# Unit 3 of a fused attention and feed-forward kernel takes the softmax-sum path of the units after it

## The chip, the cores and the metric

The kernel runs on one core of a Trainium2 chip. The metric is the device time of one execution in microseconds, given as the median of several runs. A profiled execution gives a span (first to last instruction) and a trace of every engine: TensorE (PE, with its weight loads shown as PEld), VectorE (DVE), ScalarE (ACT), GpSimd (POOL), and SyncE (SP), which only issues DMAs here.

## The reference

Attention with normalised queries and keys, for 8 batches of 12 heads, 448 tokens and 64 channels a head, and then two matrix products over the 3584 tokens:

```python
q_n, k_n = rmsnorm(q, g_q), rmsnorm(k, g_k)
scores = (1 / sqrt(64)) * q_n @ k_n.T
attn = exp(scores - max(scores))
attn = attn / (sum(attn) + 1e-9)
x = concat_heads(attn @ v)            # 3584 x 768
h = x @ w_in                          # 768 x 2048
out = maximum(0.01 * h, h) @ w_out    # 2048 x 768
```

## The kernel before

**Units and steps.** The work of attention is cut into 24 units (`NU`). A unit is four heads of one batch, so that three units make a batch; unit 3 is the first of batch 1. A unit's scores are computed transposed, as seven tiles of 128 keys by 2 x 448 (`et[:, t]`, t = 0 to 6). From unit 3 on, one loop (L963) runs over units `u` and four steps `d`: step 0 computes tile 0, steps 1 to 3 two tiles each (`STEPS`). Each tile is scored by PE into a *score slot* (`slot`, L194: two PSUM banks, two such slots in all), and ACT takes its exponential (`ex`, L218). The scores of step 0 also give the shift of the exponential: DVE takes a maximum over the tile (L236), spreads it on a diagonal `dg` (L238), a small PE matmul brings it to every partition (`shift_mm`), DVE takes the maximum of that (L249 or L255) and makes the bias `eb` (L257), for which the unit's first exponential waits.

**What closes a unit.** The closing of unit u-1 stands in step 0 of unit u. It has two forms, and `narrow(u-1)` chooses:

- The wide form (`zsum_slot`, `pv`, `zinv`, `xmul`), used before for units 0, 1, 3 and 23 (unit 2 has a variant of its own). The sums over the keys are computed by 64-row matmuls with a block of ones into a score slot, where each of 64 partitions gets the same sum (L280). PV goes to two of the four `aux` banks (L367). ACT makes the reciprocal of the sums with Ln and Exp over 128 x 896 (L353, L354), and DVE multiplies PV in PSUM by it, giving `xt`, the input of the first matrix product (L376).
- The narrow form (`pv_slot`, `zcol`, `pv_out`, `zcol_ln`, `zcol_inv`, `xmul_sb` or `xmul_pool`), used for units 4 to 22. PV goes to a score slot. The sums are computed by 32-column matmuls into one `aux` bank, as 128 x 224 (L307). The shift's matmul writes to the rest of PV's slot (L248). PV is copied to `x32` in SBUF, by DVE for units 4 to 6 and by ACT after that (L320, L322). ACT does Ln and Exp over 128 x 224 (L327, L332), and four DMAs on SyncE's queue spread the result to `rz`, 128 x 896 (L337). The product of `x32` and `rz` (L347) follows a unit or half a unit later, on DVE or on GpSimd.

**Added exponential tiles.** `add_e` (L292) lets DVE add up the first `ADDED[u]` exponential tiles of a unit in fp16. The sums then need `7 - ADDED[u] + 1` matmul groups instead of seven. `ADDED[3]` is 5: four additions, three groups.

**What sets the order.** Everything is issued in an order written by hand (`manual_schedule`); each engine takes its instructions in that order. The matrix products wait in `queue` as items of six to eight matmuls (`moe1`, L389, reading `xt`; `moe2` and `seven`, reading `gt`). `fill(u, d, jobs)` takes as many of them in each step as a digit of `PLAN` says ("1222" for unit 4) and places the step's `jobs` between them. In unit 4, step 0, `prep_tr` also transposes unit 5's normalised queries and keys on PE (L179); for units from 6 on that is a DMA transpose (`prep_trd`, L183), followed by a scaling on DVE (`prep_g`, L155).

**Preparing units ahead.** Unit u+4's rows are loaded by SyncE in step 0 (L125), their squares are made by GpSimd or ACT (L152, L148), reduced by DVE (L159), and normalised by DVE in step 2 (`prep_norm`, L171) two units ahead. SyncE's queue holds these loads, the `rz` DMAs, the DMA transposes and the stores, in program order. GpSimd's DMA queue holds the weights and the rows of v.

Of the kernel before, what the change touches and what calls it, by code (L numbers as in the profile page):

```python
# [18 lines left out]
def kernel(  # L19
# [18 lines left out]
    NU = B * NQ  # L38
# [163 lines left out]
    def qk(u, steps):  # L202
        st[u]["sT"] = []
        for t in steps:
            sT = slot()
            score(u, t, (sT[:, 0], sT[:, 1]))
            st[u]["sT"].append((t, sT))
# [17 lines left out]
    def shift_max(u):  # L225
        s = st[u]
        sT = s["sT"][0][1]
        if isinstance(sT, list):
            pm2 = small.tile([P, 2], FP32, tag="pm2", name="pm2")
            for a in range(2):  # L230
                nc.vector.tensor_reduce(pm2[:, a:a + 1], sT[a][:, 0:S], axis=AXL.X, op=ALU.max)
            s["spare"] = sT[0]
            nc.vector.tensor_reduce(s["spare"][:, 511:512], pm2, axis=AXL.X, op=ALU.max)
        else:
            s["spare"] = sT[:, 0]
            nc.vector.tensor_reduce(s["spare"][:, 511:512], sT[:, :, 0:S], axis=AXL.XY, op=ALU.max)  # L236
        s["dg"] = small.tile([P, P], FP16, tag="dg", name="dg")
        nc.vector.tensor_tensor(s["dg"], ident16, s["spare"][:, 511:512].broadcast_to([P, P]), op=ALU.mult)  # L238
# [4 lines left out]
    def shift_mm(u):  # L243
        s = st[u]
        if u > 0 and "pslot" in st[u - 1]:
            pb = st[u - 1]["pslot"][:, :, S:S + 64]
            for x in range(2):
                nc.tensor.matmul(pb[:, x], onesp, s["dg"][:, 64 * x:64 * x + 64], start=True, stop=True)  # L248
            nc.vector.tensor_reduce(s["spare"][:, 510:511], pb, axis=AXL.XY, op=ALU.max)  # L249
        else:  # L250
            if "pb" not in s:
                shift_bank(u)
            pb = s["pb"]
            nc.tensor.matmul(pb[:, 0:P], onesp, s["dg"], start=True, stop=True)
            nc.vector.tensor_reduce(s["spare"][:, 510:511], pb[:, 0:P], axis=AXL.X, op=ALU.max)  # L255
        s["eb"] = small.tile([P, 1], FP32, tag="eb", name="eb")
        nc.vector.tensor_scalar(s["eb"], s["spare"][:, 510:511], -1.0, DELTA, op0=ALU.mult, op1=ALU.add)  # L257
# [24 lines left out]

    HS = S // 2
    ADDED = {u: 4 for u in (7, 10, 11, 13, 16, 17, 19)}
    ADDED.update({3: 5, 4: 5, NU - 1: 5})
    ADDED.update({u: 3 for u in (8, 14, 20, 22)})

    def add_e(u):
        s = st[u]
# [9 lines left out]
    def zcol(u):  # L299
        s = st[u]  # L300
        s["zc"] = aux([P, 512], FP32, "zc")
        ets = z_tiles(u)
        for i, e in enumerate(ets):
            for y in range(2):
                for a in range(2):
                    c = 32 * (2 * y + a)
                    nc.tensor.matmul(s["zc"][c:c + 32, 0:HS], onesr, e[:, a, HS * y:HS * y + HS],  # L307
                                     start=(i == 0), stop=(i == len(ets) - 1))

    def pv_slot(u):  # L310
        s = st[u]
        s["pslot"] = slot()
        s["pv"] = [s["pslot"][:, r] for r in range(2)]
        pv(u)

    def pv_out(u):
        s = st[u]
        s["x32"] = zpool.tile([P, 2, S], FP32, tag="x32", name="x32")
        if u in (4, 5, 6):
            nc.vector.tensor_copy(s["x32"], s["pslot"][:, :, 0:S])  # L320
        else:
            nc.scalar.copy(s["x32"], s["pslot"][:, :, 0:S])  # L322

    def zcol_ln(u):
        s = st[u]
        s["zs"] = zpool.tile([P, HS], FP32, tag="zs", name="zs")
        nc.scalar.activation(s["zs"], s["zc"][:, 0:HS], AF.Ln)  # L327
        drop(s["zc"])
# [10 lines left out]
    def xmul_sb(u):  # L339
        xmul_pool(u, nc.vector)  # L340
# [74 lines left out]
    def flush(keep=False):  # L415
        kept = [p for p in pend if keep and p[0] in (s1, s2, s3, s4)]
        now = [p for p in pend if p not in kept]
        pend[:] = kept
        for fn, args in now:
            fn(*args)  # L420
# [312 lines left out]
    STEPS = ((0,), (1, 2), (3, 4), (5, 6))  # L733

    def narrow(u):
        return 4 <= u < NU - 1

    def fed(u, d):
        return u % NQ == 0 and d == 3
# [31 lines left out]
    with tc.manual_schedule():  # L771
# [191 lines left out]
        for u in range(3, NU):  # L963
            for d in range(4):
                if d > 0 or u > 3:
                    qk(u, STEPS[d])
                    if d == 0:
                        shift_max(u)
                        flush()
                        if u == 6:  # L970
                            xmul_sb(u - 2)
                        if narrow(u - 1):
                            pv_slot(u - 1)
                            zcol(u - 1)
                            shift_mm(u)
                            pv_out(u - 1)
                        else:
                            zsum_slot(u - 1)
                            pv(u - 1)
                            shift_mm(u)  # L980
                            zinv(u - 1)
                    ex(u)
                    if d == 0 and narrow(u - 1):
                        zcol_ln(u - 1)
                if d == 2 and ADDED.get(u, 0) > 3 and u < NU - 1:
                    add_e(u)
                    if u > 4:
                        xmul_sb(u - 1)
                jobs = []

                def job(fn, *args):
                    jobs.append(lambda: fn(*args))

                if d == 0:
                    if u == 3:
                        prep_norm(4)
                        gate(4)
                    elif narrow(u - 1):
                        if u < NU - 1:
                            job(zcol_inv, u - 1)  # L1000
                    else:
                        xmul(u - 1)
                    if u + 4 < NU:
                        job(load, u + 4)
                    if u + 3 < NU:
                        load_v(u + 3)
                    if u < 6:
                        prep_sqp(u + 3)
                if d == 1 and narrow(u - 1) and not 5 <= u < 8 and ADDED.get(u, 0) < 4:
                    xmul_pool(u - 1)  # L1010
                if u == NU - 1:
                    if d == 1:
                        job(zcol_inv, u - 1)
                if fed(u, d) and u > 3:
                    push(u // NQ - 1)
                if (u, d) in ((3, 1), (4, 0)):
                    for ti in range(2):
                        prep_tr(u + 1, ti, VV)
                if d == 1 and 5 <= u < NU - 1:
                    job(prep_g, u + 1)  # L1020
                if u + 2 < NU:
                    if d == 1:
                        if ADDED.get(u) == 3:
                            job(lambda u: (prep_ssq(u + 2), add_e(u)), u)
                        else:
                            for ti in range(2):
                                job(prep_ssq, u + 2, ALL, (ti,))
                    if d == 2:
                        job(prep_rinv, u + 2)
                        if u == 6:  # L1030
                            job(xmul_sb, u - 1)
                        for ti in range(2):
                            job(prep_norm, u + 2, ALL, (ti,))
                        if u > 3:
                            job(prep_trd, u + 2)
                if d == 1 and 4 <= u < 8:
                    job(weight_sum, u - 4, 0)
                if d == 0 and 5 <= u < 9:
                    job(weight_sum, u - 5, 1)
                if d == 1 and u == NU - 2:  # L1040
                    jobs.append(lambda: None)
                    job(add_e, u)
                if u == NU - 2 and d == 0:
                    for n, tile_ in ((1, (raws, "rq", 3)), (2, (raws, "rk", 3)), (3, None), (4, (prep_p, "sq", 3))):
                        job(win_sum, n, 1, tile_)
                    for n in (3, 1, 2, 4):
                        job(x_sum, LATE, n)
                if u == NU - 1 and d == 3:
                    job(add_e, u)
                    job(xmul_sb, u - 1)  # L1050
                if d == 3 and 6 <= u < NU - 3:
                    for ti in range(2):
                        job(prep_sq, u + 3, ALL, (ti,))
                fill(u, d, jobs)
# [39 lines left out]
```

## Time and profile before

| what | value |
|---|---|
| time, median of 3 runs | 415.95 us (415.69 to 416.95) |
| span of the profiled execution | 414.3 us |
| unit 4 begins (first score matmul) | 54.82 us |
| unit 5 begins | 68.90 us |
| unit 6 begins | 81.02 us |
| DVE busy 60.3 to 69.0 us | 8.30 of 8.70 us |
| ACT busy 60.3 to 69.0 us | 8.49 of 8.70 us |
| PE busy 60.3 to 69.0 us | 8.70 of 8.70 us |
| DMA for w_out, issue to landing | 23.5 and 33.0 us |

How to read it: the page gives each engine's share of the span, the chain of work that ended last, and groups of instructions by line. The timeline gives single instructions in order of time, with the idle time of the engine before each in brackets and what ended it. A busy engine is not always a bound: the stage around the change is what counts, and there the three compute engines are all nearly full.

### The profile page before, as it was taken

The page shows a single profiled execution, that of the slowest core. Times are in us where ns is not written, and L with a number is a line of the kernel's source. Part 1 is how long each engine was busy: PE and PEld are TensorE (multiplying, and loading weights), DVE is VectorE, ACT ScalarE, POOL GpSimd, SP SyncE. Part 2 cuts the span into 40 slices and gives each one's busy share as a digit, 9 for nine tenths or more (in the row PEclk, how much of TensorE's full clock was granted, in tenths as well). Part 3 has the DMA queues.
Part 4 walks back from the last instruction along what each step waited for, and adds up shares of the span by engine and source line. Part 5 has one row for each costly group of instructions (what it writes and reads, how often), then busy time and mean ns, then how long its engine had stood idle before and what let it go on. Part 6 is the DMA issues. An engine that isn't in the chain of part 4 may idle for free.

```text
span 414.3 us, 9374 instructions
## 1 busy us (share of the span) xinstructions
PE 399.1 (96%) x3831; PEld 219.6 (53%) x3831; DVE 308.7 (74%) x492; ACT 300.1 (72%) x470; POOL 68.4 (17%) x70
## 2 busy tenths in 40 slices
PE   8779999999999999999999999998999999999995
PEld 7445444454445544555445544454445557558863
DVE  5889798898788766767669757768568788658762
ACT  5989987667887699777987779866986657653600
POOL 1868422200020200020020200002002202000000
PEclk9999999999999999999999999999999999999998
DMA  5999999899765895677664796666562470032023
GB/s 178 290 239 251 241 250 177 207 170 214 140 156 89 221 239 92 159 194 157 163 151 77 211 212 133 171 157 128 194 112 47 120 149 18 9 77 76 2 56 97
DMA packets 71950, 62.41 MB, mean 151 GB/s; under 512 B 36324, under 2 KB 67044, under 8 KB 71908
## 3 DMA queue, kind: packets, MB, share of 16 engines
q1 hardware_dynamic: 61312, 49.62, 46.8%
q0 software_dynamic: 10272, 11.80, 18.2%
q8 instruction: 30, 0.49, 0.5%
q10 hardware_dynamic: 324, 0.39, 0.3%
q14 instruction: 12, 0.10, 0.1%
HBM read 45.61 MB, written 11.01 MB: 137 GB/s over the span
## 4 chain that ended last, share of the span: by engine, by line
PE 80%; DVE 10%; ACT 4%; DMA 2%; issue 2%; SPq 1%; DVEq 0%; ACTq 0%
PE hps L389 27%; PE sT L199 8%; PE op L435 5%; PE sT L367 5%; PE bank L602 5%; PE bank L476 5%; PE ma L476 5%; PE mc L476 4%; PE md L476 4%; DVE n L171 3%; ACT et L218 3%; PE mb L476 2%; PE zc L307 2%; PE sT L476 1%; DVE sT L236 1%
## 5 line engine op out<-in xcount | busy, mean ns | idle before, releaser
L218 ACT ACTIVATE et<-sT,eb 128x896 f16<-128x896 f32 x166 | 159.6, 1010 | 23.9 <-PE sT L199 13.9
L389 PE MATMUL hps<-xt,win 128*128 128x448 f16 x600 | 120.8, 353 | 0.2 <-DVE xt L376 0.2
L389 PEld LDWEIGHTS <-win 128*128 128x128 f16 x612 | 56.7, 98 | 58.3 <-issue 9.5
L383 ACT ACTIVATE gt<-hps 128x448 f16<-128x448 f32 x100 | 54.0, 557 | 4.7 <-PE hps L389 4.1
L199 PE MATMUL sT<-qkT 64*64 64x448 f16 x664 | 52.5, 363 | 3.0 <-ACT et L218 2.1
L159 DVE TENSOR_REDUCE ssq<-sq 128x14 f32<-128x896 f32 (+2 forms) x49 | 50.1, 1059 | 1.3 <-ACT sq L148 1.2
L476 PEld LDWEIGHTS <-sa 128*128 128x128 f16 x352 | 32.8, 98 | 26.4 <-issue 5.8
L128 POOL DMA_DIRECT2D vt<-in_v_dram x24 | 18.0, 748 | 169.3 <-PE sT L367 163.2
L322 ACT COPY x<-sT 128x896 f32<-128x896 f32 x16 | 14.5, 906 | 31.2 <-DVE sT L249 31.2
L476 PEld LDWEIGHTS <-gt 128*128 128x128 f16 x264 | 25.3, 98 | 18.4 <-issue 2.1
L199 PEld LDWEIGHTS <-qkT 64*64 64x64 f16 x672 | 15.3, 104 | 36.2 <-issue 32.0
L347 POOL TENSOR_TENSOR xt<-x,rz 128x896 f16<-128x896 f32 x9 | 18.7, 2082 | 81.7 <-DMA rz<-zs 73.5
L171 DVE TENSOR_TENSOR n<-rq,rinv 128x896 f16<-128x896 f32 (+2 forms) x25 | 28.7, 1149 | 3.4 <-ACT rinv L165 3.4
L236 DVE TENSOR_REDUCE sT<-sT 128x1 f32<-128x896 f32 x22 | 24.1, 1095 | 7.4 <-PE sT L199 7.3
L367 PE MATMUL sT<-et,vt 64*64 64x448 f16 x532 | 28.4, 349 | 0.0
L435 PE MATMUL op<-wout,gt 128*128 128x384 f16 x160 | 28.4, 327 | 0.0
L292 DVE TENSOR_TENSOR ea<-ea,et 128x896 f16<-128x896 f16 x27 | 16.9, 625 | 15.0 <-ACT et L218 13.7
L171 DVE TENSOR_TENSOR n<-rk,rinv 128x896 f16<-128x896 f32 (+2 forms) x26 | 26.2, 1012 | 0.0
L367 PEld LDWEIGHTS <-vt 64*64 64x64 f16 x672 | 20.1, 107 | 10.8 <-issue 0.4
L435 PEld LDWEIGHTS <-gt 128*128 128x128 f16 x192 | 17.7, 98 | 13.7 <-issue 3.1
L476 PE MATMUL ma<-wout,gt 128*128 128x384 f16 x128 | 23.5, 326 | 0.0
L292 DVE TENSOR_TENSOR ea<-et 128x896 f16<-128x896 f16 x14 | 9.4, 673 | 10.5 <-ACT et L218 10.5
(144 smaller groups left out, 550.5 us busy)
## 6 DMA issues: line engine op xcount, KB each, us to landing
rq<-in_q_dram SPq DMA_DIRECT2D x24, 448.0 KB, 3.9
rk<-in_k_dram SPq DMA_DIRECT2D x24, 448.0 KB, 5.0
out_dram<-ost SPq DMA_DIRECT2D x52, 192.0 KB, 3.2
rz<-zs SPq DMA_DIRECT2D x76, 112.0 KB, 2.3
vt<-in_v_dram POOLq DMA_DIRECT2D x24, 224.0 KB, 4.7
win<-in_moe_w_in_dram POOLq DMA_DIRECT2D x8, 384.0 KB, 13.8
wout<-in_moe_w_out_dram POOLq DMA_DIRECT2D x2, 1536.0 KB, 28.3
out_dram<-ost SPq DMA_DIRECT2D x4, 96.0 KB, 2.1
```

Of the source, the lines that this page charges most:

```text
L159: nc.vector.tensor_reduce(buf(u, "ssq")[:, ti, :, c[0]:c[1]], buf(u, f"sq{ti}")[:, :, c[0]:c[1]], axis=AXL.X, op=ALU.add)
L171: nc.vector.tensor_tensor(buf(u, "n16")[:, ti, c[0]:c[1]].rearrange("p s a d -> p a s d"), src[:, :, c[0]:c[1]], buf(u, "rinv")[:, ti, :, ...
L199: nc.tensor.matmul(banks[a][64 * r:64 * r + 64, 0:S].rearrange("p (t x) -> p t x", t=NS), kT(u, r, a, t), qT(u, r, a), start=True, stop=True)
L218: nc.scalar.activation(s["et"][:, t], sT[:, :, 0:S], AF.Exp, bias=s["eb"], scale=1.0)
L236: nc.vector.tensor_reduce(s["spare"][:, 511:512], sT[:, :, 0:S], axis=AXL.XY, op=ALU.max)
L292: nc.vector.tensor_tensor(s["ea"], s["et"][:, 0] if t == 1 else s["ea"], s["et"][:, t], op=ALU.add)
L367: nc.tensor.matmul(s["pv"][r][64 * a:64 * a + 64, 0:S], vts[u % NV][64 * r:64 * r + 64, a, t], s["et"][64 * r:64 * r + 64, t, a], start=(t ...
L383: nc.scalar.activation(dst, src, AF.Prelu, bias=0.0, scale=1.0, alpha=0.01)
L389: nc.tensor.matmul(hps[:, 0:S], win16[:, kt // 2, kt % 2, ts(ft, P)], xt[:, kt // 2, kt % 2], start=(kt == 0), stop=(kt == KT - 1))
L435: nc.tensor.matmul(op2[:, 0:HC], gt[:, ft, ds(col(t), P)], wout16[:, ft, ds(HC * half, HC)], start=(i == 0), stop=(i == FT - 1))
L476: nc.tensor.matmul(bank[:, 0:HC], a[:, f], b[:, f], start=(first and f == 0), stop=(f == HF - 1), skip_group_check=not first)
L602: nc.tensor.matmul(bank[:, HX * i:HX * i + HX].rearrange("p (t x) -> p t x", t=NS), w, x[:, kt], start=start, stop=(kt == HK - 1), skip_gr ...
```

## The change

Unit 3 is closed in the narrow form instead of the wide one. With it:

- `ADDED[3]` goes from 5 to 3: two additions instead of four on DVE in unit 3's step 2, five groups of sums matmuls instead of three. The place of the additions stays (step 2, ahead of the jobs).
- PV of unit 3 goes to the score slot that the wide sums used, and the sums and the shift of unit 4 no longer need the two `aux` banks of PV and the one of the shift (one `aux` bank for the sums instead).
- Unit 3's PV is copied by DVE (`pv_out` lists it), its reciprocals take the small Ln and Exp and four DMAs; the latter stand on SyncE's queue ahead of unit 8's load.
- The product for unit 3 is made by DVE in step 0 of unit 5, between `dg` and the maximum that makes `eb` (`u in (5, 6)`).

It frees DVE and ACT of work in unit 3 and at its end, and makes unit 3 the same as the units after it.

```diff
-    ADDED.update({3: 5, 4: 5, NU - 1: 5})
-    ADDED.update({u: 3 for u in (8, 14, 20, 22)})
+    ADDED.update({4: 5, NU - 1: 5})
+    ADDED.update({u: 3 for u in (3, 8, 14, 20, 22)})
...
-        if u in (4, 5, 6):
+        if u in (3, 4, 5, 6):
             nc.vector.tensor_copy(s["x32"], s["pslot"][:, :, 0:S])
...
     def narrow(u):
-        return 4 <= u < NU - 1
+        return 3 <= u < NU - 1
...
-                        if u == 6:
+                        if u in (5, 6):
                             xmul_sb(u - 2)
...
-                if d == 2 and ADDED.get(u, 0) > 3 and u < NU - 1:
+                if d == 2 and (u == 3 or ADDED.get(u, 0) > 3) and u < NU - 1:
                     add_e(u)
...
-                        if ADDED.get(u) == 3:
+                        if ADDED.get(u) == 3 and u > 3:
                             job(lambda u: (prep_ssq(u + 2), add_e(u)), u)
```

## The prediction

> **What bounds the kernel now.** I read the page's busy shares and the shares of the chain that ended last first.
>
> ```profile
> PE 399.1 (96%) x3831; PEld 219.6 (53%) x3831; DVE 308.7 (74%) x492; ACT 300.1 (72%) x470; POOL 68.4 (17%) x70
> ...
> PE 80%; DVE 10%; ACT 4%; DMA 2%; issue 2%; SPq 1%; DVEq 0%; ACTq 0%
> ```
>
> TensorE (PE) works 96% of the span and carries 80% of the chain. An edit can therefore win only PE work that it removes and PE idle time that it closes. The view of waits for PE gives little idle time after 50 us: 0.58 and 0.18 us where unit 4 begins, 0.34 us at 190.8, 1.13 us at 286.4 and 0.15 us at 393.7. The change lies at the first two. So next comes the timeline (start, us, engine, line, operation, and in brackets the idle time before it) where unit 4 takes over from unit 3:
>
> ```profile
> 54.20 1.08 DVE L171 TENSOR_TENSOR n<-rq,rinv 128x896 f16<-128x896 f32 x1
> 54.82 0.38 PE L199 MATMUL sT<-qkT 64*64 64x448 f16 x4
> 55.03 0.55 PE L280 MATMUL sT<-et,ones 64*64 64x448 f16 x8
> 55.41 0.36 PE L280 MATMUL sT<-ea,ones 64*64 64x448 f16 x4
> 55.60 1.49 PE L367 MATMUL pv<-et,vt 64*64 64x448 f16 x28
> 56.20 1.09 DVE L236 TENSOR_REDUCE sT<-sT 128x1 f32<-128x896 f32 x1
> 57.33 0.29 DVE L238 TENSOR_TENSOR dg<-ident,sT 128x128 f16<-128x128 f16 x1
> 57.67 0.23 PE L254 MATMUL pb<-dg,onesp 128*128 128x128 f16 x1 [0.58 <-DVE dg L238]
> 59.02 1.31 PE L389 MATMUL hps<-xt,win 128*128 128x448 f16 x6 [0.18 <-DVE xt L376]
> ```
>
> PE finishes unit 3's sums and PV near 57.1 and waits for dg. VectorE (DVE) is late because it ends the second normalisation only at 56.28, behind four additions (50.76 to 54.28); the maximum L236 could have run when the score of 54.82 was done. The second wait, 0.18 us, is for a PSUM bank that unit 3's PV held until the product L376 had read it.
>
> The same hand-over, with the path that unit 3 is to take, is in units 5 (12 sums matmuls) and 6 (28):
>
> ```profile
> 68.90 0.38 PE L199 MATMUL sT<-qkT 64*64 64x448 f16 x4
> 69.11 1.49 PE L367 MATMUL sT<-et,vt 64*64 64x448 f16 x28
> 70.53 0.38 PE L307 MATMUL zc<-et,onesr 128*32 128x224 f16 x8
> 70.94 0.23 PE L248 MATMUL sT<-dg,onesp 128*128 128x64 f16 x2
> 71.62 1.08 DVE L320 COPY x<-sT 128x896 f32<-128x896 f32 x1
> 71.80 1.01 ACT L218 ACTIVATE et<-sT,eb 128x896 f16<-128x896 f32 x1 [2.21 <-DVE eb L257]
> 73.50 2.60 SPq L337 DMA_DIRECT2D rz<-zs  x4
> 76.20 0.54 SPq L125 DMA_DIRECT2D rq<-in_q_dram  x1
> 82.66 0.85 PE L307 MATMUL zc<-et,onesr 128*32 128x224 f16 x28
> 83.35 1.08 DVE L347 TENSOR_TENSOR xt<-x,rz 128x896 f16<-128x896 f32 x1
> ```
>
> It supplies the offsets used below: scores to PV 0.21 us, PV to sums 1.42, twelve sums 0.41, twenty-eight 0.82, matmul of the shift to the exponential 0.86, to the end of the x copy 1.76.
>
> **What the Trainium skill says.** "ScalarE: Activation LUTs", section What ACT_TABLE_LOAD costs, prices an activation without a pointer operand at 186 ns + 0.833 ns per element: 373 ns for 224 and 932 for 896. The trace agrees: 0.35 and 0.39 us (L327, L332), 0.92 and 0.95 (L353, L354). "TensorE: Matmul & The Clock Gate", section Architectural detail, calls VectorE's queue strict first-in first-out. The trace fits: L236 waits behind normalisations that it does not need. "DMA: Bandwidth & Descriptors", section Queues, rings and completion order, says that a DMA engine alternates between queues packet by packet and takes each ring in order. The DMA view by the microsecond agrees: between 59 and 64 us the GpSimd queue moves 77 to 86 packets in each, and the SyncE queue 77 to 84.
>
> **The change part by part.**
>
> DVE loses two additions, 0.73 us apart on their chain, so 1.4 us. The first addition still ends at 52.09 and the second near 52.8; rinv is ready at 52.41. The normalisations then run 52.8 to 54.9 instead of 54.2 to 56.3. L236 now waits only for its score: 54.82 + 0.50 (unit 5: 68.90 to 69.40) = 55.32. dg is ready at 55.32 + 1.42 = 56.74.
>
> PE: twelve 64-row sums (0.57 us) become twenty 32-column sums. Between twelve for 0.41 and twenty-eight for 0.82, twenty cost 0.61. So PV starts at 55.03, the sums at 56.45, the shift matmuls at 57.06. dg has been ready 0.3 us by then, so the wait of 0.58 is gone. The 14 transposes take 0.96 after 0.07, and L389 starts at 58.09 instead of 59.02. Its bank is not PV's any more. Sum: 0.58 + 0.18 of waits, 0.13 of drain and transposes' pauses, 0.04 of sums back, about 0.08 of rounding: **0.93 us**.
>
> PSUM slot: the second score of step 1 (PE at 60.26 - 0.93 = 59.33) needs the slot that PV now holds. It is free when the x copy ends, 57.06 + 1.76 = 58.82; the first score's slot when the exponential ends, 57.06 + 0.86 + 1.01 = 58.93. Both are 0.4 us early: nothing lost, hidden by the transposes and six matmuls.
>
> ScalarE (ACT) loses 0.92 + 0.95 and gains 0.35 + 0.39, but the 0.39 moves behind the next Prelu. The exponentials of step 1 then start at 60.28, 0.4 late against everything else's shift; about 0.2 is left of this at step 2, as the Prelu there waited for PE 0.22 anyway. Step 2's scores at 62.21 need slots free at 61.2 and 62.1. Nothing lost, with 0.1 to 0.3 us to spare.
>
> DVE in unit 4 swaps two products from PSUM (1.15) for the x copy (1.08). In unit 5 it gains the product L347 (1.08), behind dg and ahead of eb. Unit 6 has it there already: shift matmul at 83.44, exponential at 84.93, an offset of 1.49 instead of 0.86. L347 hides part of itself behind PE's sums, so I cost 0.55 us on the exponential. ACT waited 0.67 us there for step 1's score (74.14). Unit 5's next exponential would be ready at 73.12, its score arrives at 73.22: nothing lost, by 0.1 us.
>
> DMA: four transfers for rz (2.60 us of issue, 2.3 each to land) are new and stand in SyncE's queue ahead of unit 8's load. They wait for the Exp at 60.3. So the load leaves at 63.0 instead of 55.3. It is wanted by GpSimd's square (71.7 before), so by itself it has time. rz is wanted by L347 near 69.8. In this stretch the first packet came 3.5 us after the issue (55.31 to 58.8); some 510 packets (four transfers; 220 a microsecond moved alone at 75 us) at 100 to 128 a microsecond beside the other queue end near 68. It holds, with 1 to 2 us. Behind them queues the transpose for unit 6 (L183). Before, the queues ran empty at 69.2, it was issued at 68.99, sent its first packets at 70.1 and landed at 73.5. After, 2.3 us of rz work is added and the load is late; I estimate the queues empty between 70.3 and 71, and so its landing at 73.8 to 74.5. DVE wants it for L155 at 75.15 - 0.93 = 74.2. Behind L155 stand the squares' sums, a weight sum, the normalisations and unit 6's maximum without a gap, and PE waits for that maximum at 83.4 with no slack. So every microsecond L155 waits is lost. That it does wait elsewhere is shown by the view of line L183, among those who waited for it:
>
> ```profile
>   DVE qkT L155: 6.5, 7
> ```
>
> Seven of 18 transposes were waited for, 6.5 us in all. I take a stall of 0; the bounds are 0 and 1.3 us.
>
> **The rivals.**
> - *Full gain, 415.0 us (chance 0.45).* 415.95 - 0.93. For it: each step has a measured template; against it: the 0.1 us margins.
> - *More, 414.3 (0.26).* Later waits for dg (0.34 and 1.13 us) hang on GpSimd's product overlapping a normalisation: L171 takes 1.95 and 2.74 us there instead of 1.08, the product having been released by an rz landing at 279.8. A shifted DMA order may undo one: 0.93 + 0.34 to 1.13. Against it: all engines shift alike.
> - *The transpose is late, 415.7 (0.17).* 0.7 us of stall leaves 0.2.
> - *Slower, 417.5 (0.12).* If the SyncE queue gets the poorer share seen at 36 to 38 us (22 packets in two microseconds), rz and the transpose land 2 to 3 us late. L347 then stops eb, or L155 stops unit 6's maximum: -0.93 + 2.5 = +1.6. For it: PE has no slack behind either; against it: the shares were equal in 59 to 64.
>
> **How the numbers follow.** The likeliest is 415.0. It lies within 0.3% (414.7 to 417.2), but 0.3 us from the edge, and the runs before spread from 415.69 to 416.95; a quarter of this case (0.11) I count as faster. With most of the second case (0.25): faster 0.36. Slower is the last case: 0.12. The rest is 0.52. The range goes from 413.9 (the second case with the larger wait gone) to 416.8 (a stall of 1.8), with some 0.1 left out on either side.
>
> **What would show it.** Right: no wait of L248 for dg in unit 4, L389 about 3.3 us after unit 4's score (58.09 - 54.82) instead of 4.2, and PE 0.9 us earlier from there to the end. Wrong: a wait of L155 for the DMA near 74 us; of L347 for rz near 70; PE waiting for a score slot at 59 or 62; or 0.2 us or more at the first exponentials of unit 5's step 1. Waits for dg at 190 and 286 that shrink or grow would make the prediction wrong in either direction.

## The result, and the profile after

The changed kernel takes 414.1 us (median; 413.82 to 414.55) beside 416.27 us for the kernel before: a ratio of 0.9948, 95% interval 0.9929 to 0.9967, so 1.4 to 3.0 us faster. The median gain is 2.2 us. The span of the profiled execution falls from 414.3 to 412.4 us.

The page of the changed kernel, busy shares and shares of the chain that ended last:

```profile
PE 398.8 (97%) x3840; PEld 220.1 (53%) x3840; DVE 307.4 (75%) x490; ACT 298.4 (72%) x470; POOL 68.4 (17%) x70
...
PE 86%; DVE 8%; ACT 3%; DMA 1%; issue 1%; DVEq 0%
```

PE's work is the same to 0.3 us; what shrank is the rest: PE's share of the chain that ended last rises from 80% to 86%. The timeline of the changed kernel where unit 4 takes over from unit 3 (start, us, engine, line; idle time before in brackets):

```profile
53.68 1.08 DVE L171 TENSOR_TENSOR n<-rk,rinv 128x896 f16<-128x896 f32 x1
54.76 0.38 PE L199 MATMUL sT<-qkT 64*64 64x448 f16 x4
54.97 1.49 PE L367 MATMUL sT<-et,vt 64*64 64x448 f16 x28
55.26 1.10 DVE L236 TENSOR_REDUCE sT<-sT 128x1 f32<-128x896 f32 x1 [0.50 <-PE sT L199]
56.40 0.57 PE L307 MATMUL zc<-et,onesr 128*32 128x224 f16 x16
56.40 0.29 DVE L238 TENSOR_TENSOR dg<-ident,sT 128x128 f16<-128x128 f16 x1
56.99 0.23 PE L248 MATMUL sT<-dg,onesp 128*128 128x64 f16 x2
57.84 1.30 PE L389 MATMUL hps<-xt,win 128*128 128x448 f16 x6
```

VectorE now waits for PE (0.50 us before L236) and no longer the other way round. The matmul of the shift has no wait, L389 has none, and L389 starts 3.08 us after the score (54.76 to 57.84) instead of 4.20 (54.82 to 59.02 before). That is **1.12 us** won in this one place.

The next two units of the changed kernel:

```profile
68.23 2.67 SPq L183 DMA_TRANSPOSE qkT<-n  x1
69.55 1.08 DVE L347 TENSOR_TENSOR xt<-x,rz 128x896 f16<-128x896 f32 x1
71.13 1.01 ACT L218 ACTIVATE et<-sT,eb 128x896 f16<-128x896 f32 x1 [2.68 <-DVE eb L257]
72.95 3.81 ACT L218 ACTIVATE et<-sT,eb 128x896 f16<-128x896 f32 x4
74.18 0.45 DVE L155 TENSOR_SCALAR qkT<-qkT,gcol 128x896 f16<-128x896 f16 x1
82.51 0.22 PE L248 MATMUL sT<-dg,onesp 128*128 128x64 f16 x2 [0.19 <-DVE dg L238]
```

L347 finds rz there: it has no wait, and its 1.08 us are the usual length. Unit 5's first exponential comes later after the shift's matmul than before, but those of step 1 (72.95) follow without a wait that the view shows. The transpose for unit 6 takes 2.67 us to issue instead of 1.63 before, VectorE stands 0.14 us before L155 (the operation before it ends at 73.09 + 0.95), and PE waits 0.19 us for dg at unit 6. So 0.90 us of the 1.12 are left at unit 6. But the spans differ by 1.9 us. Most of the rest comes much later. The timeline of the kernel before around units 18 and 19:

```profile
279.83 2.07 POOL L347 TENSOR_TENSOR xt<-x,rz 128x896 f16<-128x896 f32 x1 [9.03 <-DMA rz<-zs]
280.12 2.74 DVE L171 TENSOR_TENSOR n<-rq,rinv 128x896 f16<-128x896 f32 x1
282.78 1.08 DVE L171 TENSOR_TENSOR n<-rk,rinv 128x896 f16<-128x896 f32 x1
286.37 0.22 PE L248 MATMUL sT<-dg,onesp 128*128 128x64 f16 x2 [1.13 <-DVE dg L238]
```

And of the changed kernel:

```profile
278.15 2.08 POOL L347 TENSOR_TENSOR xt<-x,rz 128x896 f16<-128x896 f32 x1 [8.71 <-DMA rz<-zs]
278.75 2.43 DVE L171 TENSOR_TENSOR n<-rq,rinv 128x896 f16<-128x896 f32 x1
281.11 1.08 DVE L171 TENSOR_TENSOR n<-rk,rinv 128x896 f16<-128x896 f32 x1
284.69 0.22 PE L248 MATMUL sT<-dg,onesp 128*128 128x64 f16 x2 [0.82 <-DVE dg L238]
```

GpSimd's product and the first normalisation collide in both. In both, L171 ends 0.95 to 0.96 us after the product ends, however early it began. An undisturbed L171 takes 1.08 us, so nearly all of its work comes after the product: it is held until GpSimd is done. In the changed kernel the product begins 0.60 us ahead of L171 instead of 0.29, and PE's wait is 0.31 us shorter. In unit 12 the same pair cost PE 0.34 us (at unit 13) before and nothing after. I call these two the *collisions*.

To compare kernels I take the starts of the shift's matmul (L254 or L248) of four units from each trace and give the distances: unit 3 to 5 (the change itself), 5 to 6 (the new product and the transpose), 6 to 23 (everything later).

| kernel | 3 to 5 | 5 to 6 | 6 to 23 | time, median us |
|---|---|---|---|---|
| before | 29.04 | 12.54 | 270.49 | 416.27 |
| after | 27.92 | 12.76 | 269.78 | 414.10 |

The three differences are -1.12, +0.22 and -0.71 us, together -1.61. Of the other 0.3 us of the span, 0.07 are gained before unit 3's shift, where nothing of the change has run yet, and some 0.2 behind the last addition to an output tile.

### The profile page after: what moved, and what is told of

Read it like the earlier page. It is cut to its first block, busy times and chain, and to the rows that moved or that the text cites. A ratio compares the mean times of both kernels' runs of the same rounds, so it can differ in the third digit from the quotient of the medians.

```text
span 412.4 us, 9399 instructions
## 1 busy us (share of the span) xinstructions
PE 398.8 (97%) x3840; PEld 220.1 (53%) x3840; DVE 307.4 (75%) x490; ACT 298.4 (72%) x470; POOL 68.4 (17%) x70
## 4 chain that ended last, share of the span: by engine, by line
PE 86%; DVE 8%; ACT 3%; DMA 1%; issue 1%; DVEq 0%
PE hps L389 28%; PE sT L199 9%; PE sT L367 5%; PE ma L476 5%; PE mc L476 5%; PE bank L602 5%; PE bank L476 5%; PE md L476 5%; PE op L435 4%; PE mb L476 3%; PE zc L307 2%; DVE n L171 2%; PE warm L769 2%; PE sT L476 1%; DMA qkT<-n 1%; ACT et L218 1%
## 5 line engine op out<-in xcount | busy, mean ns | idle before, releaser
L389 PE MATMUL hps<-xt,win 128*128 128x448 f16 x600 | 120.8, 353 | 0.0
L389 PEld LDWEIGHTS <-win 128*128 128x128 f16 x612 | 56.7, 98 | 57.9 <-issue 9.9
L347 POOL TENSOR_TENSOR xt<-x,rz 128x896 f16<-128x896 f32 x9 | 18.9, 2094 | 82.0 <-DMA rz<-zs 82.0
L171 DVE TENSOR_TENSOR n<-rq,rinv 128x896 f16<-128x896 f32 (+2 forms) x25 | 27.7, 1112 | 3.4 <-ACT rinv L165 3.4
L236 DVE TENSOR_REDUCE sT<-sT 128x1 f32<-128x896 f32 x22 | 24.1, 1094 | 8.1 <-PE sT L199 8.0
L367 PE MATMUL sT<-et,vt 64*64 64x448 f16 x560 | 29.9, 349 | 0.0
L292 DVE TENSOR_TENSOR ea<-ea,et 128x896 f16<-128x896 f16 x25 | 15.6, 626 | 15.1 <-ACT et L218 14.2
L171 DVE TENSOR_TENSOR n<-rk,rinv 128x896 f16<-128x896 f32 (+2 forms) x26 | 26.1, 1012 | 0.0
L148 ACT ACTIVATE sq<-rq 128x896 f32<-128x896 f32 (+2 forms) x18 | 16.3, 913 | 1.2 <-DMA rq<-in_q_dram 1.2
```

Source lines behind the costliest of these rows:

```text
L171: nc.vector.tensor_tensor(buf(u, "n16")[:, ti, c[0]:c[1]].rearrange("p s a d -> p a s d"), src[:, :, c[0]:c[1]], buf(u, "rinv")[:, ti, :, ...
L347: eng.tensor_tensor(xts[b][:, g], s["x32"], s["rz"], op=ALU.mult)
L367: nc.tensor.matmul(s["pv"][r][64 * a:64 * a + 64, 0:S], vts[u % NV][64 * r:64 * r + 64, a, t], s["et"][64 * r:64 * r + 64, t, a], start=(t ...
L389: nc.tensor.matmul(hps[:, 0:S], win16[:, kt // 2, kt % 2, ts(ft, P)], xt[:, kt // 2, kt % 2], start=(kt == 0), stop=(kt == KT - 1))
```

## The experiments

**Theory A:** the change gains directly some 0.9 to 1.1 us at units 3 to 6; the further gain is a collision that turned out milder, and depends on when rz lands. **Rival B:** the change itself acts on the later units. **Rival C:** one part of the change (the additions, or the path) makes the gain alone.

### The two kernels again

No edit; a second trace and more runs of each.

> The kernel before, unchanged, looked at a second time. Theory A (direct gain of 0.9 us at units 3 to 5 and a further 0.7 us because two collisions of GpSimd's product with a normalisation, at units 12 and 18, differ by how fast the rz DMAs get out): the ratio is 1.000, but the waits for dg at units 13 and 19 (0.34 and 1.13 us in the first trace) come out different by some tenths, and DVE's first normalisation in units 12 and 18 with them, while the wait at unit 4 is 0.58 again. Rival B (the later waits are set by the change itself): 0.34 and 1.13 us again, within 0.05.

> The changed kernel, unchanged, looked at a second time. Theory A: no wait at unit 4, 0.2 us at unit 6, a shift of about 0.9 us at unit 6 against the kernel before; the waits at units 13 and 19 (0 and 0.82 us in the first trace) differ by some tenths; time 0.995 of before, 414 us. Rival B: 0 and 0.82 again, within 0.05, and the same 414 us.

| kernel | 3 to 5 | 5 to 6 | 6 to 23 | wait at 13, 19 | median us | ratio to before |
|---|---|---|---|---|---|---|
| before again | 29.04 | 12.54 | 270.23 | 0, 1.29 | 416.40 | 1.0009 (0.9998 to 1.0019) |
| after again | 27.92 | 12.55 | 269.55 | 0, 0.59 | 413.94 | 0.9954 (0.9941 to 0.9967) |

The distance 3 to 5 comes back to the hundredth: 1.12 us are the change's own. The wait at unit 6 was 0.19 in one trace and 0 in the other. The waits at units 13 and 19 do vary within one kernel (0.34 and 0; 1.13 and 1.29; 0.82 and 0.59), which is against B in its strict form. The missing wait at unit 13 can't be put down to the change: the kernel before has that wait in one trace and not in the other.

### One part alone

Additions alone: the kernel before with `ADDED[3] = 3`, the wide path kept (and the additions kept in step 2, ahead of the jobs, as in the changed kernel).

```diff
-    ADDED.update({3: 5, 4: 5, NU - 1: 5})
-    ADDED.update({u: 3 for u in (8, 14, 20, 22)})
+    ADDED.update({4: 5, NU - 1: 5})
+    ADDED.update({u: 3 for u in (3, 8, 14, 20, 22)})
```

> The kernel before with two additions instead of four in unit 3 and five groups of wide sums instead of three; everything else stays, the wide path too. Both theories: dg is ready near 56.7, PE gets to the shift's matmul at 57.4 to 57.5 (0.38 us more of sums), so the wait of 0.58 goes but 0.4 of it is paid back in sums; L389 starts at 58.8 to 58.9 instead of 59.02. Gain 0.1 to 0.2 us at unit 5, time 415.8 to 416.2. If the additions alone were the cause of the gain it would show 0.9 us at unit 5.

Its timeline:

```profile
54.35 0.38 PE L199 MATMUL sT<-qkT 64*64 64x448 f16 x4
56.94 0.23 PE L254 MATMUL pb<-dg,onesp 128*128 128x128 f16 x1
58.35 1.31 PE L389 MATMUL hps<-xt,win 128*128 128x448 f16 x6 [0.24 <-DVE xt L376]
```

Path alone: the changed kernel with `ADDED[3] = 5`.

```diff
-    ADDED.update({4: 5, NU - 1: 5})
-    ADDED.update({u: 3 for u in (3, 8, 14, 20, 22)})
+    ADDED.update({3: 5, 4: 5, NU - 1: 5})
+    ADDED.update({u: 3 for u in (8, 14, 20, 22)})
```

> The changed kernel with the four additions of before, and so three groups of 32-column sums. Both theories: PE is through with PV and sums at 56.8 and waits 0.7 to 0.8 us for dg at 57.6; the bank's wait is gone; L389 starts at 58.5 to 58.7 instead of 59.02 (before) and 57.84 (after). Gain 0.3 to 0.4 us at unit 5 instead of 1.1. If the path alone were the cause it would show 0.9 or more.

Its timeline:

```profile
54.26 0.38 PE L199 MATMUL sT<-qkT 64*64 64x448 f16 x4
57.11 0.22 PE L248 MATMUL sT<-dg,onesp 128*128 128x64 f16 x2 [0.74 <-DVE dg L238]
57.95 1.30 PE L389 MATMUL hps<-xt,win 128*128 128x448 f16 x6
```

| kernel | 3 to 5 | 5 to 6 | 6 to 23 | wait at 13, 19 | median us | ratio to before |
|---|---|---|---|---|---|---|
| additions alone | 28.83 | 12.55 | 270.32 | 0, 1.37 | 415.08 | 0.9979 (0.9970 to 0.9988) |
| path alone | 28.51 | 12.56 | 270.98 | 0.93, 1.04 | 415.56 | 0.9993 (0.9977 to 1.0008) |

C falls. The additions alone gain 0.21 us from unit 3 to unit 5, the path alone 0.53 (expected 0.3 to 0.4), both together 1.12, more than the sum. The stretch from unit 4's first score to L389 shows why, in two halves:

| kernel | score to shift's matmul | shift's matmul to L389 | both |
|---|---|---|---|
| before | 2.85 | 1.35 | 4.20 |
| additions alone | 2.59 | 1.41 | 3.99 |
| path alone | 2.85 | 0.84 | 3.68 |
| after | 2.23 | 0.85 | 3.08 |

In the first half the parts need each other. The additions alone have dg early, so the wait for it is gone, but the five groups of wide sums take longer. The path alone has short sums, and waits just that much longer for dg: 0.74 instead of 0.58 us. Only both together have an early dg and short sums.

The second half is the path's alone, and at 0.5 us it is more than the 0.18 us that the trace gives as idle. With the wide path two things hold PE up there. The eighth of the 14 transposes starts 0.22 us after the seventh instead of 0.055, just when L255 has read the shift's bank. And L389 starts 0.40 us (before) after the last transpose instead of 0.06; more than half of this the trace counts as busy, as it gives each transpose 0.22 us. That the transposes wait for the shift's bank is read from these times; no run tests it by itself.

The additions alone were timed 1.1 us below the kernel before (415.08 beside 416.22 in the same set; 415.8 to 416.2 was expected), though their trace shows only 0.21 of it and has the longest wait of all at unit 19. That made me doubt A, and so the next runs take the collisions away.

### Without the collisions

GpSimd's products for units 11 and 17 are moved from step 1 to the end of step 2 of the next unit, behind a one-element copy that reads the second normalised operand:

```diff
-                if d == 1 and narrow(u - 1) and not 5 <= u < 8 and ADDED.get(u, 0) < 4:
+                if d == 1 and narrow(u - 1) and not 5 <= u < 8 and u not in (12, 18) and ADDED.get(u, 0) < 4:
                     xmul_pool(u - 1)
...
                 fill(u, d, jobs)
+                if d == 2 and u in (12, 18):
+                    gate(u + 2)
+                    xmul_pool(u - 1)
```

> The kernel before, with GpSimd's products for units 11 and 17 moved from step 1 of units 12 and 18 to the end of step 2, behind a one-element copy that reads the second normalised operand, so that they can't overlap the two normalisations. Theory A (the collision makes the waits for dg at units 13 and 19, and their size is chance of the rz DMAs): both waits are gone, L171 takes 1.08 us everywhere, the time falls by the mean of the waits, 0.2 to 0.5 and 1.2 us, to 414.5 to 414.9 us, 0.996 to 0.997. Rival B (these waits come from a DVE queue that is too full in those units whatever GpSimd does): they stay within 0.3 us, time 416.

> The changed kernel with the same two products moved. Theory A: no wait at units 13 and 19; time falls by some 0.7 us to 413.2, and the distance to the kernel before with the same move is the direct gain alone, 0.9 to 1.1 us (0.0025), not the 2.2 us between the kernels without it. Rival B (the change acts on later units by another way, through the order of DMAs or of the queues): the distance stays near 2.0 us, with a gain at units 13 to 23 that no wait for dg explains.

And, in a later set beside each other, all four kernels (before, additions alone, path alone, after) with this edit:

> The kernel before with the two moved products, again, as the base of a comparison of four without the two collisions. All theories: 414.1 to 414.8 us, 0.9945 to 0.9965 of the kernel before, wait of 0.58 for dg at unit 4 and none after.

> Two additions fewer alone, with the two moved products. Theory A (away from the collisions only units 3 to 6 differ, as in the traces): 0.2 us less than the kernel before with the moved products. Rival B (fewer additions gain more elsewhere, as the 0.9 to 1.1 us by which it was timed faster without the moves would have it): 0.7 us or more less.

> The path alone, with four additions and the two moved products. Theory A: 0.5 us less than the kernel before with the moved products, a wait of 0.74 for dg at unit 4. Rival: 0 or 1 us less.

> The changed kernel with the two moved products, again. Theory A: 0.9 to 1.1 us less than the kernel before with the moved products, so more than the two parts alone together (0.2 and 0.5). Rival B: 1.5 us or more less.

| kernel, products moved | 3 to 5 | 5 to 6 | 6 to 23 | median us | ratio to before |
|---|---|---|---|---|---|
| before | 29.05 | 12.54 | 268.91 | 414.09 | 0.9953 (0.9940 to 0.9966) |
| after | 27.92 | 12.70 | 268.91 | 412.98 | 0.9925 (0.9912 to 0.9937) |
| before, later set | 29.04 | 12.54 | 268.91 | 413.93 | 0.9948 (0.9933 to 0.9962) |
| additions alone, later set | 28.84 | 12.54 | 268.90 | 414.09 | 0.9947 (0.9934 to 0.9960) |
| path alone, later set | 28.52 | 12.99 | 268.89 | 413.59 | 0.9940 (0.9926 to 0.9954) |
| after, later set | 27.92 | 13.07 | 268.91 | 413.29 | 0.9943 (0.9919 to 0.9967) |

The view of waits for PE from 44 to 410 us, of the kernel before with the products moved:

```profile
PE pb L254 <- DVE dg L238: 0.6, 1, 0.6
PE sT L397 <- DVE xt L376: 0.5, 1, 0.5
PE hps L389 <- DVE xt L376: 0.2, 1, 0.2
PE sT L476 <- DVE sa L460: 0.2, 1, 0.2
```

And of the changed kernel with the products moved:

```profile
PE sT L397 <- DVE xt L376: 0.5, 1, 0.5
PE sT L476 <- DVE sa L460: 0.2, 1, 0.2
```

The two lines that are missing in the second are the two waits that the change removes. From unit 6 to 23 all six traces agree to 0.02 us: without the collisions nothing in that stretch tells the kernels apart. So the gain beyond units 3 to 6 lies in the collisions, as A has it. Whether the change itself makes them milder, which would be a weak form of B, this does not settle (see "What stays open"). With the collisions, that stretch was 1.58 and 1.32 us longer in the traces of the kernel before and 0.87 and 0.64 in those of the changed kernel. In time, after and before with the products moved are 1.11 us apart in one set and 0.64 in the other (A expected 0.9 to 1.1), instead of 2.2 and 2.3 with the collisions (416.27 - 414.10, and 416.22 - 413.94 in the set of the second traces). The additions alone show no gain that can be told from zero (414.09 beside 413.93): the 1.1 us timed before were not the additions' direct gain, and no trace shows where they came from.

Moving the two products is worth as much as the change: the kernel before gains 2.3 and 2.2 us by it in its two sets (to 414.09 and 413.93; 414.5 to 414.9 was expected).

The later set also shows the transpose. In its changed kernel:

```profile
67.94 2.93 SPq L183 DMA_TRANSPOSE qkT<-n  x1
...
74.20 0.45 DVE L155 TENSOR_SCALAR qkT<-qkT,gcol 128x896 f16<-128x896 f16 x1 [0.45 <-DMA qkT<-n]
...
82.53 0.22 PE L248 MATMUL sT<-dg,onesp 128*128 128x64 f16 x2 [0.50 <-DVE dg L238]
```

0.45 us of wait at L155 came out as 0.50 at PE eight microseconds later. Over the four traces of the changed kernel, with and without the edit, the distance 5 to 6 is 0.22, 0.01, 0.16 and 0.53 us longer than 12.54, and what is left of the 1.12 is 0.90, 1.11, 0.97 and 0.59 (distance 3 to 6 against 41.58 or 41.59 before). The path alone has the new DMAs too, and in the later set its 5 to 6 was 0.45 us longer. Such a stall may be why before and after lie closer in that set than in the first, but one traced run for each kernel doesn't show it.

### Unit 8's load ahead of rz

In unit 4, step 0, SyncE's queue gets the load first and the four rz DMAs after it, to have the transpose for unit 6 find the queue empty:

```diff
+                    if u == 4:
+                        job(load, 8)
                     if u == 3:
                         prep_norm(4)
...
-                    if u + 4 < NU:
+                    if u + 4 < NU and u != 4:
                         job(load, u + 4)
```

> The changed kernel with unit 8's load ahead of unit 3's four rz DMAs on SyncE's queue in unit 4. Both theories: the load leaves near 54 us instead of 62.7, the transpose for unit 6 is issued at about 68.2 in 1.6 us instead of 2.7 and lands before 73.5; L155 follows the weight sum at once (0.14 to 0.2 us of idle gone) and PE's wait of up to 0.19 us at unit 6 is gone. rz lands a little later, still before L347 (69.5). Gain 0 to 0.2 us against the changed kernel. If rz became late instead, L347 would wait and the exponential of unit 5 with it.

Its timeline:

```profile
54.24 0.37 SPq L125 DMA_DIRECT2D rq<-in_q_dram  x1
...
60.48 2.59 SPq L337 DMA_DIRECT2D rz<-zs  x4
...
70.19 0.76 POOL L128 DMA_DIRECT2D vt<-in_v_dram  x1 [7.11 <-PE sT L367]
70.31 3.31 DVE L347 TENSOR_TENSOR xt<-x,rz 128x896 f16<-128x896 f32 x1 [0.22 <-DMA rz<-zs]
70.97 1.69 POOL L152 TENSOR_TENSOR sq<-rq 128x896 f32<-128x896 f32 x1
73.54 0.28 DVE L249 TENSOR_REDUCE sT<-sT 128x1 f32<-128x128 f32 x1
75.17 0.61 PE L199 MATMUL sT<-qkT 64*64 64x448 f16 x8 [2.14 <-ACT et L218]
```

And GpSimd at the same place in the changed kernel, where L347 starts at 69.55:

```profile
69.73 0.76 POOL L128 DMA_DIRECT2D vt<-in_v_dram  x1 [7.11 <-PE sT L367]
70.52 1.69 POOL L152 TENSOR_TENSOR sq<-rq 128x896 f32<-128x896 f32 x1
```

The expected gain was wrong; the last sentence of the expectation is what happened, though the wait for rz is the smaller part of it. rz now queues behind the load and takes a median 7.2 us from issue to landing (6.0 in the changed kernel). L347 waits only 0.22 us for it, but then occupies VectorE for 3.31 us instead of 1.08, and eb stands behind it. It ends at 73.62, 0.96 us after GpSimd's square L152 (72.66): the mark of the collisions in units 12 and 18. In the changed kernel L347 starts 0.18 us ahead of GpSimd's v load, which the square follows at once; here it starts 0.12 us behind it. So a small lateness loses a place, and the lost place costs 2.2 us. Whether the v load's issue already holds L347, or only the square does, the trace doesn't tell.

ScalarE and then PE lose 2.14 us at once; unit 3 to unit 6 takes 44.15 us, more than the 41.58 of the kernel before. The runs scatter from 413.6 to 417.87 us, median 415.64, 0.9984 (0.9969 to 1.0000) of the kernel before; the traced one is among the slowest, and the fastest is as fast as the changed kernel. So the gain of the change hangs on L347 getting its rz before GpSimd's next work begins, and the place of the rz DMAs on the queue decides how often it does. The transpose did not get faster either: its issue took 2.99 us.

With both edits:

> The changed kernel with both moves (unit 8's load first, the two products behind the normalisations). Theory A: 413.0 us, 0.9925 of the kernel before; no wait of PE for dg after unit 3. Rival B: no better than the changed kernel, 414.

L347 takes 3.23 us and again ends 0.96 us after the square; unit 3 to 6 takes 42.70; 6 to 23 takes 268.92, as without collisions. The median is 414.68 us (413.0 was expected), 0.9958 (0.9942 to 0.9975): worse than the moved products alone, for the same reason. The best version is the changed kernel with the two products moved, 412.98 and 413.29 us in its two sets, ratios 0.9925 and 0.9943.

## Why the prediction was right or wrong

The time lies in the stated range, and the direct mechanism at units 3 to 6 is the one that was forecast. But the gain, 2.2 us, is more than twice the likeliest one (0.95), and slightly more than the largest in the range (415.95 - 413.9 = 2.05); the time is inside it because the kernel before was timed at 416.27 this time. "Within 0.3%" had been given 0.52, "faster" 0.36, and faster it was. What happened was the second case ("More", 414.3).

- **Additions and dg: right.** Foreseen: L236 with no wait but its score's, dg ready before PE. Seen: L236 at 55.26 after a wait of 0.50 for the score, dg at 56.69, PE's shift matmul 2.23 us after the score (foreseen 57.06 - 54.82 = 2.24).
- **Transposes: mis-sized.** I took 0.96 us for the fourteen, which is how long they are shown busy; L389 follows 0.78 us after the first (57.06 to 57.84). That is 0.18 of the 0.19 us by which the direct gain, 1.12 us, exceeds the 0.93. The trace before had the right figure: unit 4's own transposes start at 47.04 and the next L389 at 47.84.
- **Score slots and ScalarE: right.** Step 1's score came at 59.07 without a wait, step 2's at 61.95 too.
- **L347 ahead of eb: right.** The exponential came 1.38 us after the shift matmul (69.75 to 71.13) instead of 0.86 (foreseen 0.86 + 0.55), and step 1's score was still the later one. The template was misread by a little: 83.44 is the start of the weight load, the matmul starts at 83.48, and unit 6's offset is 1.45.
- **The transpose: right about the place, too good about the value.** I chose a stall of 0 within 0 to 1.3 us; units 5 to 6 took 0.01 to 0.53 us more, 0.23 in the mean of four traces. It is luck that this about cancels the 0.19 us above, so that the 0.90 us left in the first trace look like the 0.93 foreseen.
- **rz in time: right, and with the margin that was named (1 to 2 us).** The last of the four was issued at 62.0 and took 6.4 us to land, the longest of them, so it was there at 68.4, 1.1 us ahead of L347. Turning the order round used it up, and gave the outcome of the fourth case. That L347 would then also be held by GpSimd's square, which makes most of the cost, was not foreseen.
- **The later waits: the step that failed.** Against the second case I set "all engines shift alike", and so kept the waits at units 13 and 19 at 0.34 and 1.13 us. They are not constants of the kernel. The prediction named how they come about; it had one trace and took its values for fixed. The runs put the cost of the collisions in the stretch from 6 to 23 at 0.6 to 2.1 us (against the 268.91 without them), and moving two products took it to 0 in every trace. By the times, that step is worth 1.1 to 1.6 us, the difference of the gain with the collisions and without.

**What stays open.** In the seven traces with the collision, the head start of GpSimd's product before L171 in unit 18 was 0.29, 0.13, 0.06 and 0.37 us in the kernels before, before again, additions alone and path alone, and 0.60, 0.83 and 0.94 in after, after again and load first. L171 keeps its place (9.91 to 9.92 us after unit 18's shift in both traces of each kernel), and the product waits for rz, so it is rz that lands earlier. So the changed kernel does seem to have the milder collision, and the times (2.2 us apart with the collisions, 0.6 to 1.1 without) say so as well. Why rz lands some tenths earlier there, 190 us after the last instruction that differs, the runs don't show. The four rz issues of that unit took 2.59 us in both traces of the kernel before, 3.70 and 3.47 in those of the changed one and 4.10 with the additions alone, which had the worst collision; so the duration of issue is not it.

And four of the 41 timed runs of the changed kernel, with and without the products moved, took 3.0 to 3.4 us more than their median (417.34 and 417.07; 416.58 and 416.31). That is about what the lost place of L347 cost in the experiment with the load first (unit 3 to 6 in 44.15 us instead of 40.5 to 41.0), but none of the four was traced.

## What to carry to other kernels

Where the bound engine's own work and another engine's result end close to each other, making one of them shorter wins only up to the other: each half of this change gave 0.2 or 0.5 us, both together 1.1. A wait seen in one trace behind work that a DMA releases is a sample and not a constant; look at two traces before its size goes into a forecast, or move the released work to where it can't collide. When a new DMA joins an in-order queue, its place against the bulk loads is part of the change: here one exchange of order cost more than the whole direct gain. And a margin is to be taken against everything that starts next, not against the consumer alone: a wait of 0.2 us for rz became a loss of more than 2 us because GpSimd's work came in between.

## What the runs showed of the hardware that I had not expected

- An operation of VectorE on two SBUF inputs doesn't run beside GpSimd's arithmetic once that has the lead. In unit 18 PE's wait plus the head start of GpSimd is the same in all seven traces: 1.13 + 0.29, 1.29 + 0.13, 1.37 + 0.06, 1.04 + 0.37, 0.82 + 0.60, 0.59 + 0.83 and 0.49 + 0.94, all 1.41 to 1.43 us. The held instruction ends 0.95 to 0.96 us after GpSimd's, for L171 behind a product and for L347 behind a square alike. Two operations with one input in PSUM are not held: L376 and L483 take their usual 0.62 and 0.56 us in the middle of GpSimd's work (27.31 and 184.85 in the kernel before). The Trainium skill, "SBUF — State Buffer", section Who interferes with whom, says that a VectorE instruction with two SBUF inputs contends with a GpSimd instruction that reads SBUF, and that the order of issue decides who blocks; the traces agree, though L347's recorded start lies ahead of the square and behind only the v load's issue. The prediction would have read the 1.95 and 2.74 us of L171 better with it.
- Outside the waits, the trace repeats to 0.02 us over 269 us of work (unit 6 to 23) in six executions of four kernels.
- A 112 KB DMA that lands in 2.3 us (median over the kernel) took a median 6.0 us beside the weight load, and 7.2 behind a 2 x 448 KB load as well.
